# A gated feed-forward stage run in passes of 768 tokens, with fewer weights narrowed in the expert stage before it

## The chip, the cores and the metric

One core of one Trainium2 chip runs the whole program. The metric is the device time of one execution in microseconds; a profiled execution also has a span, the stretch from the first to the last recorded instruction.

## The reference

Three layers follow each other on 2304 tokens of 512 numbers (4 sequences of 576 tokens, 8 heads of 64):

```python
# 1: attention with exponential features (d_feat = 128)
proj = einsum('bhsd,df->bhsf', x, w_phi); proj -= max(abs(proj))
phi = concatenate([exp(proj), exp(-proj)])
num = einsum('bhsf,bhfd->bhsd', phi(q), einsum('bhsf,bhsd->bhfd', phi(k), v))
x = num / (einsum('bhsf,bhf->bhs', phi(q), phi(k).sum(2)) + 1e-6)
# 2: one of 8 experts per token (w1: 512 x 1024, w2: 1024 x 512)
logits = x @ w_gate + modality_bias[modality_id]; e = argmax(logits)
x = gate[e] * (maximum(x @ w1[e], 0) @ w2[e])
# 3: gated stage (w_a, w_b: 512 x 1536, w_out: 1536 x 512)
out = ((x @ w_a) * (x @ w_b)) @ w_out
```

Inputs of attention and of the experts are fp32. The weights of the gated stage come as float64 and are brought to fp32 on the chip, which the kernel calls narrowing.

## The kernel before

**Precision.** Every large product is made of three matmuls in the fp32r format. An operand is split into a rounded part (`...h`, a copy on ScalarE) and a rest (`...l`, a subtraction on VectorE or GpSimd). `mm3` (L51) then adds high by high, high by rest and rest by high: lines L52, L53 and L54 of the profile.

**Attention** (class `Attn`) works in 8 units and writes its result to a DRAM buffer `xs`. While it runs, `Route` sorts the tokens of the first half by expert. Its last matmuls are `nmp` (L236).

**The expert stage** (class `Moe`) works on 4 tiles, two for each half of the tokens. A tile is 608 gathered tokens with the same expert. It has 8 steps (`NJ`), each with 1/8 of the expert's weights and 48 matmuls of 304 columns: steps 0 to 3 make the hidden layer (`l1`, result `hp`, split into `hh` and `hl`, L588 and L589), steps 4 to 7 the second layer (`l2`, result `yp`, copied into `y`, L601). In each step:

- `loadw` (L540) brings raw weights `s` by SP's queue, three buffers (`p_st`); three loads are asked for at the start, and each split asks for the load three steps on.
- `splitw` (L545) makes `wh` on ScalarE (L550) and `wl` (L551) on VectorE in steps 0 to 3, on GpSimd in steps 4 to 7. It is emitted two steps before the weights are used.
- `gather` (L554) fetches 128 tokens by an indirect DMA that GpSimd issues (L559) into one of three buffers (`p_xg`); five make a tile. `transp` (L562) turns them on TensorE (`mxt`, L571) and splits them into `mxh` (ScalarE, L574) and `mxl` (VectorE, L575). The next tile's transposes lie in steps 4 to 7, so the first tile is the only one whose gathers and transposes stand ahead of all expert matmuls.
- `side` holds extra work by step: routing the second half (steps 0 to 6), `close_work` (step 7, gives scratch memory to the narrowing), and from step 8 on `conv(f)` (L901) for ten of the twelve groups (`NPRE = 10`) of gated-stage weights. A group is three pieces of 128x512. `narrow` (L676) takes seven VectorE operations for a piece (L681 to L690) on one pair of scratch tiles, `cvt` and `cvs`; the result `cvo` is stored to the DRAM buffer `wsc`. Groups 0 and 1 are also split here for the first two steps of the next stage. `conv` has a low priority (`LOWP`).

**Between the stages** stands `tc.If(nts[2] > NTMIN)` (L911), for inputs that need more than two tiles in a half. Here it isn't taken, but every engine branches there.

**The gated stage** (class `Moe2`) goes over 6 blocks of 384 tokens and, for each, over 12 groups of weights `f`: 72 steps of 33 matmuls. In a step `ab` (L745) makes two products `abp` (24 matmuls of 384 columns), then `ga` (ScalarE), `gg` (VectorE, L761), `gh` (ScalarE, L762) and `gl` (VectorE, L763); `outp` (L766) of the step before adds to three accumulators `op` (9 matmuls of 512 columns), kept over the 12 groups. `split` (L722) splits the weights of every step anew, 210 pieces in all: `fh` on ScalarE (L728), `fl` (L729) on VectorE for two pieces and on GpSimd for the third. The results `abp` have two buffers each in PSUM (`ps_l2`), the accumulators take three banks. `block` (L733) splits a block of `y` into `yh` and `yl` in the middle of the block before; the first one is split at the head of this stage, behind the If. The two groups that were not narrowed before are narrowed in the first block, and the others are read back from `wsc`. `finish` (L784) scales the result and writes it out by indirect DMA.

**What sets the order.** Code is emitted in the order of these loops; the Tile framework's scheduler then orders each engine's instructions by dependencies and priorities (`LOWP` and `LOWP2` lower the priority of narrowing) and decides on the semaphores. SP's queue carries loads and stores, GpSimd's queue the gathers and the output.

Of the kernel before, what the change touches and what calls it, by code (L numbers as in the profile page):

```python
# [37 lines left out]
NPRE = 10  # L38
CVK = 3
# [478 lines left out]
class Moe:  # L518
    NJ = 8

    def __init__(self, nc, tc, ctx, cst, xs, wm, y, ps_l, ps_t):
# [81 lines left out]
    def run(self, tiles, side={}):  # L603
# [12 lines left out]
        def split(k):  # L616
            if k < NT * NJ:
                self.splitw(get(k // NJ), k % NJ)
                load(k + 3)

        for j in range(3):
            self.gather(get(0), j)
        for k in range(3):
            load(k)
        split(0)
        for j in range(NSUB):
            self.transp(Ts[0], j)
            if j + 3 < NSUB:
                self.gather(Ts[0], j + 3)
        split(1)  # L630
        order = {4: (0,), 5: (1, 2), 6: (3,), 7: (4,)}
        for k in range(NT * NJ):
# [5 lines left out]
            if n + 1 < NT:  # L638
                if j == 2:
                    for i in range(3):  # L640
                        self.gather(get(n + 1), i)
                for i in order.get(j, ()):
                    self.transp(Ts[n + 1], i)
                    if i + 3 < NSUB:
                        self.gather(Ts[n + 1], i + 3)
# [7 lines left out]
class Moe2:  # L653
    NF = FF2 // P

    def __init__(self, nc, tc, w, wsc, y, routes, out, p_w, f64):
        self.nc, self.tc, self.w, self.y, self.routes, self.out = nc, tc, w, y, routes, out
        self.wsc = wsc
        self.p_w, self.f64 = p_w, f64
# [3 lines left out]
    def pools(self, ctx, ps_a, ps_l):  # L663
        tc = self.tc
        pool = lambda n, b: ctx.enter_context(tc.tile_pool(name=n, bufs=b, side="right", reuse_waits="tile"))
        self.p_y = pool("f_y", 6)
# [25 lines left out]
    def early(self, f, pool):  # L692
        nc = self.nc
        tiles = []
        for i in range(3):
            dst = pool.tile([P, 512], F32, tag=f"o{i}", name="cvo")
# [5 lines left out]
            tiles.append(dst)  # L702
        return tiles
# [18 lines left out]
    def split(self, srcs):  # L722
        nc = self.nc
        out = []
        for i, src in enumerate(srcs):
            hi = self.p_w.tile([P, 512], F32R, tag=f"h{i}", name=f"fh{i}")
            lo = self.p_w.tile([P, 512], F32R, tag=f"l{i}", name=f"fl{i}")
            nc.scalar.copy(hi, src)  # L728
            (nc.vector if i < 2 else nc.gpsimd).tensor_sub(lo, src, f32(hi))  # L729
            out.append((hi, lo))  # L730
        return out

    def block(self, bp, blk, n):  # L733
        nc = self.nc
        src = self.y[bp][:, :, blk * n:blk * n + n]
        res = []
        for c in range(4):
            yh = self.p_y.tile([P, n], F32R, tag="h", name="yh")
            yl = self.p_y.tile([P, n], F32R, tag="l", name="yl")
            nc.scalar.copy(yh, src[:, c, :])  # L740
            nc.vector.tensor_sub(yl, src[:, c, :], f32(yh))
            res.append((yh, yl))
# [31 lines left out]
    def run(self, ws, side):  # L774
        nc = self.nc
        n = 384
        blocks = [(bp, b) for bp in range(2) for b in range(HALF // n)]
        y = self.block(*blocks[0], n)
        seq = [(i, f) for i in range(len(blocks)) for f in range(self.NF)]
        prev = None  # L780
        ys = {0: y}
        accs = {}

        def finish(i):  # L784
            bp, b = blocks[i]
# [16 lines left out]
        def second(k):  # L802
            i, f = seq[k]
            if f == 0:
                accs[i] = [self.ps_a.tile([P, 512], F32, tag=f"a{m}", name=f"op{m}") for m in range(n // P)]
            self.outp(gs.pop(k), ws.pop(k), accs[i], f)
# [3 lines left out]
        gs = {}  # L810
        for k, (i, f) in enumerate(seq):
# [25 lines left out]
def trn_kernel(ctx, tc, qk, v, w_phi, mod_id, w_gate, bias, wm, wf, out):  # L837
# [35 lines left out]
    with ExitStack() as mctx:  # L873
# [3 lines left out]
        p_w = ctx.enter_context(tc.tile_pool(name="f_w", bufs=2, **tl))  # L877
        y = [ypool.tile([P, 4, YC], F32, name=f"y{i}") for i in range(2)]
# [107 lines left out]
```

## Time and profile before

| what | value |
|---|---|
| median of 3 runs | 940.4 us (938.87, 940.4 and 945.45) |
| the profiled execution | 943.89 us, its span 942.1 us |
| matmuls, and other instructions | 5861 on TensorE, 15371 in all |
| attention | 0 to about 232 us |
| expert stage, first to last matmul | 240.90 to 471.28 us |
| gated stage, first to last matmul | 477.74 to 934.23 us |

The profile gives for each engine the time in which it was busy, and for TensorE the clock that was granted, as a share of full speed (1.00 is 2.4 GHz, 0.50 is 1.2 GHz; a value between is a mean over a stretch). A busy share tells which engine could be the bound. Which wait costs time is read from the waits and the timeline of a stretch: in brackets stands how long the engine was idle before an instruction and which engine, operand and line ended it. PE is TensorE's matmuls, DVE is VectorE, ACT is ScalarE, POOL is GpSimd; a `q` behind a name is that engine's sequencer.

### The profile page before, as it was taken

Reading aid. Unit: us, or ns where it says so; the run is one execution under the profiler, and the core shown is the slowest. Engines: PE = TensorE matmul, PEld = TensorE weight load, DVE = VectorE, ACT = ScalarE, POOL = GpSimd, SP = SyncE. Lnnn points to the kernel's source line nnn. Section 1 sums busy time; section 2 is a strip of 40 time slices with the busy share of each in tenths; the row PEclk is TensorE's granted clock in tenths of the full one; section 3 lists DMA queues with packets and bytes.
Section 4 is the critical chain, followed back from the end, with each engine's and each line's share of the span. In section 5 each row is a group of like instructions: output and inputs, shape, how many; then the busy total and the mean of one; then the engine's idle time right before and its main releaser. Section 6 shows DMA issues by size and latency. Waiting matters only on the chain. (4 is left out here: it accounts for less than half of the span.)

```text
span 942.1 us, 15371 instructions
## 1 busy us (share of the span) xinstructions
PE 907.3 (96%) x5861; PEld 864.1 (92%) x5861; DVE 622.9 (66%) x1212; ACT 436.2 (46%) x800; POOL 257.3 (27%) x235
## 2 busy tenths in 40 slices
PE   7999999899999989899979999999999999999996
PEld 5899998899999989899979999999999999999996
DVE  7978899979657999999958753353344335334431
ACT  5676765656334433233134454454444445445442
POOL 5444332302241331302103232213213223223122
PEclk7999998799999999899989999999999999999999
DMA  7232330023336566675475000000000000000000
GB/s 249 98 104 79 102 104 13 28 80 106 123 109 205 178 224 204 213 223 180 146 264 198 23 23 12 1 1 34 0 1 35 1 1 34 1 1 34 1 1 34
DMA packets 36291, 81.68 MB, mean 87 GB/s; under 512 B 4688, under 2 KB 14368, under 8 KB 36208
## 3 DMA queue, kind: packets, MB, share of 16 engines
q1 hardware_dynamic: 33168, 70.85, 23.2%
q0 software_dynamic: 3040, 9.75, 3.1%
q8 instruction: 48, 0.79, 0.3%
q14 instruction: 35, 0.29, 0.1%
HBM read 63.29 MB, written 17.30 MB: 86 GB/s over the span
## 5 line engine op out<-in xcount | busy, mean ns | idle before, releaser
L728 ACT CAST fh<-wr 128x512 fp32r<-128x512 f32 x210 | 130.3, 621 | 221.2 <-PE abp L53 147.1
L729 DVE TENSOR_TENSOR fl<-wr,fh 128x512 fp32r<-128x512 f32 x140 | 100.0, 715 | 184.3 <-ACT fh L728 176.2
L52 PE MATMUL abp<-yh,fh 128*128 128x384 f32 x576 | 194.4, 340 | 6.2 <-ACT yh L740 6.2
L53 PE MATMUL abp<-yl,fh 128*128 128x384 f32 x576 | 195.2, 339 | 0.0
L54 PE MATMUL abp<-yh,fl 128*128 128x384 f32 x576 | 194.6, 338 | 0.0
L729 POOL TENSOR_TENSOR fl<-wr,fh 128x512 fp32r<-128x512 f32 x70 | 93.3, 1333 | 340.0 <-ACT fh L728 300.8
L52 PEld LDWEIGHTS abp<-yh,fh 128*128 128x128 f32 x576 | 108.8, 189 | 9.4 <-ACT yh L740 6.4
L53 PEld LDWEIGHTS abp<-yl,fh 128*128 128x128 f32 x576 | 108.6, 189 | 3.0
L54 PEld LDWEIGHTS abp<-yh,fl 128*128 128x128 f32 x576 | 108.6, 188 | 0.0
L52 PE MATMUL op<-fh,gh 128*128 128x512 f32 x216 | 85.5, 396 | 0.0
L53 PE MATMUL op<-fl,gh 128*128 128x512 f32 x216 | 85.1, 394 | 0.0
L54 PE MATMUL op<-fh,gl 128*128 128x512 f32 x216 | 84.5, 394 | 0.0
L53 PE MATMUL yp<-hl,wh 128*128 128x304 f32 x256 | 79.1, 309 | 3.5 <-DVE hl L589 3.5
L52 PE MATMUL yp<-hh,wh 128*128 128x304 f32 x256 | 78.9, 308 | 0.0
L54 PE MATMUL yp<-hh,wl 128*128 128x304 f32 x256 | 78.4, 306 | 0.0
L761 DVE TENSOR_TENSOR gg<-abp,ga 128x384 f32<-128x384 f32 x72 | 40.1, 556 | 57.9 <-PE abp L54 57.5
L53 PE MATMUL hp<-mxl,wh 128*128 128x304 f32 x256 | 77.4, 302 | 0.0
L52 PE MATMUL hp<-mxh,wh 128*128 128x304 f32 x256 | 77.2, 303 | 0.0
L54 PE MATMUL hp<-mxh,wl 128*128 128x304 f32 x256 | 76.8, 300 | 0.0
L236 PE MATMUL nmp<-kx,qts 128*128 128x73 f32 (+1 forms) x640 | 73.4, 271 | 1.9 <-DVE grest L478 1.8
L236 PEld LDWEIGHTS nmp<-kx,qts 128*128 128x128 f32 (+1 forms) x640 | 69.8, 187 | 4.2 <-issue 3.2
L551 POOL TENSOR_TENSOR wl<-s,wh 128x1024 fp32r<-128x1024 f32 x16 | 41.5, 2595 | 110.4 <-ACT wh L550 97.6
(191 smaller groups left out, 1930.6 us busy)
## 6 DMA issues: line engine op xcount, KB each, us to landing
raw<-in_moe_w SPq DMA_DIRECT2D x36, 512.0 KB, 4.6
s<-in_moe_w SPq DMA_DIRECT2D x32, 512.0 KB, 4.2
wsc<-cvo SPq DMA_DIRECT2D x30, 256.0 KB, 4.6
wr<-wsc SPq DMA_DIRECT2D x30, 256.0 KB, 5.4
v<-in_v SPq DMA_DIRECT2D x8, 640.0 KB, 5.3
qk<-in_qk SPq DMA_DIRECT2D x7, 640.0 KB, 5.0
qk<-in_qk SPq DMA_DIRECT2D x8, 512.0 KB, 6.0
xs<-x SPq DMA_DIRECT2D x16, 256.0 KB, 2.5
```

Of the source, the lines that this page charges most:

```text
L52: nc.tensor.matmul(out, lh, rh, start=start, stop=False)
L53: nc.tensor.matmul(out, lh, rl, start=False, stop=False)
L54: nc.tensor.matmul(out, ll, rh, start=False, stop=stop)
L236: nc.tensor.matmul(ps[pp, o, :], qt[:, c, a, pp], st["kx", b][:, 2 * h + c, :], start=c == 0, stop=c == 1)
L551: (nc.gpsimd if j >= 4 else nc.vector).tensor_sub(lo, src, f32(hi))
L728: nc.scalar.copy(hi, src)
L729: (nc.vector if i < 2 else nc.gpsimd).tensor_sub(lo, src, f32(hi))
L761: nc.vector.tensor_mul(g, pss[1][:, :n], a)
```

## The change

- **Gated stage in passes.** A pass takes two blocks, 768 tokens. The loops run over pass, group and the block within the pass, so weights are split once for a pass and used for two steps: 108 pieces in place of 210. The steps stay 72 of 33 matmuls.
- **PSUM.** Two blocks need six banks of accumulators; `abp` is left with one buffer each (`ps_l2`, 2 to 1).
- **Rests on VectorE.** `wl` of steps 4 to 7 and the third `fl` of each step go from GpSimd to VectorE.
- **Narrowing.** Six groups, not ten, are narrowed in the expert stage; the other six (18 pieces) follow in the first pass, one piece after each step or nearly so. The scratch there has one buffer, not two. `cvo` has two buffers for all pieces, and the pieces of groups 0 and 1 are split as soon as each is made.
- **Buffers.** The raw expert weights (`p_st`) and the gathers (`p_xg`) have two buffers each in place of three; loads and gathers are asked for two ahead. The next tile's transposes 0 and 1 lie in step 4, 2 in step 5.
- **The first block of y** is split ahead of the If, into a pool of 8 buffers that is made early; inside the If, behind the extra tiles, it is split again. The other blocks are split at the first step that needs them or, at a pass's end, ahead of it.

```diff
-NPRE = 10
-CVK = 3
+NPRE = 6
...
-        self.p_st = pool("m_st", 3, **r)
+        self.p_st = pool("m_st", 2, **r)
-        self.p_xg = pool("m_xg", 3, **r)
+        self.p_xg = pool("m_xg", 2, **r)
...
-        (nc.gpsimd if j >= 4 else nc.vector).tensor_sub(lo, src, f32(hi))
+        nc.vector.tensor_sub(lo, src, f32(hi))
...
-                load(k + 3)
+                load(k + 2)
-        for j in range(3):
+        for j in range(2):
             self.gather(get(0), j)
-        for k in range(3):
+        for k in range(2):
             load(k)
         split(0)
         for j in range(NSUB):
             self.transp(Ts[0], j)
-            if j + 3 < NSUB:
-                self.gather(Ts[0], j + 3)
+            if j + 2 < NSUB:
+                self.gather(Ts[0], j + 2)
         split(1)
-        order = {4: (0,), 5: (1, 2), 6: (3,), 7: (4,)}
+        order = {3: (), 4: (0, 1), 5: (2,), 6: (3,), 7: (4,)}
...
-            (nc.vector if i < 2 else nc.gpsimd).tensor_sub(lo, src, f32(hi))
+        nc.vector.tensor_sub(lo, src, f32(hi))
...
-        seq = [(i, f) for i in range(len(blocks)) for f in range(self.NF)]
+        seq = [(p, f, i) for p in range(0, nb, 2) for f in range(self.NF) for i in (p, p + 1)]
...
-        for k, (i, f) in enumerate(seq):
+        for k, (p, f, i) in enumerate(seq):
             with self.tc.high_priority(offset=-LOWP2):
                 for st in side.get(k, ()):
                     st()
-            if k + 1 < len(seq) and k + 1 not in ws:
-                ws[k + 1] = self.split(self.res[seq[k + 1][1]])
-            if f == 6 and i + 1 < len(blocks):
-                ys[i + 1] = self.block(*blocks[i + 1], n)
-            gs[k] = self.ab(ys[i], ws[k])
+            if i == p + 1 and k + 1 < len(seq):
+                nxt = seq[k + 1][:2]
+                if nxt not in ws:
+                    ws[nxt] = [self.split(j, src) for j, src in enumerate(self.res[nxt[1]])]
+                if nxt[0] != p:
+                    ys[p + 2] = self.block(p + 2)
+            if i not in ys:
+                ys[i] = self.block(i)
+            gs[k] = self.ab(ys[i], ws[p, f])
...
         mo.run(tiles, side)
+        ys = {0: m2.block(0)}
         with tc.If(nts[2] > NTMIN):
             for rt, nt in zip(routes, nts):
                 extra(tc, mo, rt, nt)
+            m2.block(0, ys[0])
         rctx.close()
-    cv.append(ctx.enter_context(tc.tile_pool(name="cv2", bufs=2, **tl)))
+    cv.append(ctx.enter_context(tc.tile_pool(name="cv2", bufs=1, **tl)))
...
-    for f in range(2, NPRE):
-        side.setdefault(max(f - 4, 0), []).extend(late[f])
-    for f in range(2):
-        side.setdefault(8, []).extend(late[f])
-    for j, st in enumerate(late[f] for f in range(NPRE, Moe2.NF)):
-        side.setdefault((j * CVK) // 2 + 1, []).extend(st)
+    for f in range(NPRE):
+        side.setdefault(2 * f - 4 if f > 1 else 16, []).extend(late[f])
+    for f in range(NPRE, Moe2.NF):
+        n = len(late[f])
+        for i, st in enumerate(late[f]):
+            side.setdefault(1 + 3 * (f - NPRE) + 3 * i // n, []).append(st)
...
-    ps_l = ctx.enter_context(tc.tile_pool(name="ps_l2", bufs=2, space=PSUM, **tl))
+    ps_l = ctx.enter_context(tc.tile_pool(name="ps_l2", bufs=1, space=PSUM, **tl))
```

The line numbers of the changed kernel are 1 lower from L52 to the expert stage's end and a few lower behind it (L571 becomes L570, L729 becomes L725, L761 becomes L756).

Three places show what the scheduler makes of it. The first is TensorE's row where attention ends and the expert stage begins: `nmp` are attention's last matmuls, `mxt` the transposes of the gathered tokens (4 per gather), `hp` the first expert matmul. Before:

```order
L236 MATMUL nmp<-kx,qts 128x73 x5
L571 MATMUL mxt<-ident,xg 128x128 x8
L236 MATMUL nmp<-kx,qts 128x73 x8
L571 MATMUL mxt<-ident,xg 128x128 x4
L236 MATMUL nmp<-kx,qts 128x73 x8
L236 MATMUL nmp<-kx,qts 64x73 x8
L571 MATMUL mxt<-ident,xg 128x128 x4
L571 MATMUL mxt<-ident,xg 128x96 x4
L52 MATMUL hp<-mxh,wh 128x304
```

And the same place now:

```order
L235 MATMUL nmp<-kx,qts 128x73 x5
L570 MATMUL mxt<-ident,xg 128x128 x8
L235 MATMUL nmp<-kx,qts 128x73 x16
L570 MATMUL mxt<-ident,xg 128x128 x8
L235 MATMUL nmp<-kx,qts 64x73 x8
L570 MATMUL mxt<-ident,xg 128x96 x4
L51 MATMUL hp<-mxh,wh 128x304
```

The third and the fourth gather are turned behind 16 more matmuls of attention, where it was 8 and 24, and 8 matmuls of attention stand between the fourth and the last, which may only be fetched when the third has been turned.

The second is GpSimd's row through the first half of the expert stage, with its gathers (`xg`) and the rests `wl`. Before:

```order
L559 DMA xg<-xs_63,idx_2902 128x512 x4
L559 DMA xg<-xs_63,idx_2902 96x512
L559 DMA xg<-xs_63,idx_2902 128x512 x3
L551 TENSOR_TENSOR wl<-s,wh 128x1024 x2
L559 DMA xg<-xs_63,idx_2902 128x512
L551 TENSOR_TENSOR wl<-s,wh 128x1024
L559 DMA xg<-xs_63,idx_2902 96x512
L551 TENSOR_TENSOR wl<-s,wh 128x1024
```

Now nothing stands between the gathers of the four tiles:

```order
L558 DMA xg<-xs_63,idx_2898 128x512 x4
L558 DMA xg<-xs_63,idx_2898 96x512
L558 DMA xg<-xs_63,idx_2898 128x512 x4
L558 DMA xg<-xs_63,idx_2898 96x512
L558 DMA xg<-xs_64,idx_3928 128x512 x4
L558 DMA xg<-xs_64,idx_3928 96x512
```

GpSimd does no arithmetic here any more; what it did stands in VectorE's row.

The third is VectorE's row over one step in the gated stage's narrowing, from one product `gg` to the next; `wr` is a narrowed piece, `fl` a rest of weights, `cvs` and `cvt` the scratch. Before:

```order
L761 TENSOR_TENSOR gg<-abp,ga 128x384
L690 TENSOR_TENSOR wr_2_14776<-cvt,cvs 128x512
L729 TENSOR_TENSOR fl_15218<-wr_1_14766,fh_15217 128x512
L687 TENSOR_SCALAR cvs<-cvt 128x512
L763 TENSOR_TENSOR gl<-gg,gh 128x384
L681 TENSOR_SCALAR cvs<-raw 128x512
L688 SCALAR_TENSOR_TENSOR cvs<-raw,cvs 128x512
L682 TENSOR_SCALAR cvs<-cvs 128x512
L690 TENSOR_TENSOR wr_0_14777<-cvt,cvs 128x512
L729 TENSOR_TENSOR fl_15285<-wr_0_14768,fh_15284 128x512
L683 TENSOR_SCALAR cvt<-cvs 128x512
L761 TENSOR_TENSOR gg<-abp,ga 128x384
```

Now:

```order
L756 TENSOR_TENSOR gg<-abp,ga 128x384
L684 SCALAR_TENSOR_TENSOR cvt<-raw,cvt 128x512
L758 TENSOR_TENSOR gl<-gg,gh 128x384
L686 TENSOR_SCALAR cvs<-cvt 128x512
L687 SCALAR_TENSOR_TENSOR cvs<-raw,cvs 128x512
L725 TENSOR_TENSOR fl_14849<-wr_2_14619,fh_14848 128x512
L689 TENSOR_TENSOR wr_0_14632<-cvt,cvs 128x512
L680 TENSOR_SCALAR cvs<-raw 128x512
L725 TENSOR_TENSOR fl_14964<-wr_0_14620,fh_14963 128x512
L681 TENSOR_SCALAR cvs<-cvs 128x512
L682 TENSOR_SCALAR cvt<-cvs 128x512
L756 TENSOR_TENSOR gg<-abp,ga 128x384
```

The mixture of narrowing, rests and `gg` is much the same; but it lasts for 18 narrowings where there were 6, and the operations of two pieces no longer alternate.

## Rows read from the trace of the kernel before

**Rows 1.** The page's first part: busy us, share of the span, instructions.

```profile
PE 907.3 (96%) x5861; PEld 864.1 (92%) x5861; DVE 622.9 (66%) x1212; ACT 436.2 (46%) x800; POOL 257.3 (27%) x235
```

**Rows 2.** Stretches: us, then PE, PEld, DVE, ACT, POOL busy (x), PEclk, DMA, GB/s.

```profile
332.00:344.00 12.00, 9.98 (x72) 9.55 (x72) 11.60 (x17) 5.12 (x9) 6.56 (x5) 1.00 0.69 224
...
380.00:392.00 12.00, 8.86 (x58) 8.61 (x57) 11.76 (x21) 3.04 (x6) 3.50 (x3) 0.88 0.53 171
392.00:404.00 12.00, 12.00 (x78) 12.00 (x77) 11.59 (x18) 2.77 (x6) 3.31 (x2) 0.83 0.64 209
...
476.00:488.00 12.00, 10.26 (x49) 10.27 (x50) 5.16 (x10) 5.25 (x12) 0.00 (x0) 0.78 0.79 276
...
554.00:630.00 76.00, 76.00 (x399) 71.10 (x398) 31.95 (x53) 35.73 (x67) 18.81 (x16) 1.00 0.03 11
```

**Rows 3.** Waits of TensorE, 188 to 500 us: us in total, times, longest.

```profile
PE yp L53 <- DVE hl L589: 3.5, 2, 3.1
...
PE mxt L571 <- DVE mxl L575: 2.0, 1, 2.0
```

**Rows 4.** Timeline, 384 to 390 us: start, us, engine line operation [idle before].

```profile
384.70 3.29 DVE L685 SCALAR_TENSOR_TENSOR cvt<-raw,cvt 128x512 int32<-128x512 int32 x1
...
385.06 2.38 POOL L551 TENSOR_TENSOR wl<-s,wh 128x1024 fp32r<-128x1024 f32 x1
...
387.92 0.46 DVE L589 SCALAR_TENSOR_TENSOR hl<-hp,hh 128x304 fp32r<-128x304 f32 x1
...
389.88 0.62 PE L53 MATMUL yp<-hl,wh 128*128 128x304 f32 x1 [3.14 <-DVE hl L589]
```

**Rows 5.** Timeline, VectorE from 456 to 461 us: the last operations of two narrowings.

```profile
456.50 0.69 DVE L690 TENSOR_TENSOR cvo<-cvt,cvs 128x512 f32<-128x512 f32 x1
...
460.52 0.69 DVE L690 TENSOR_TENSOR cvo<-cvt,cvs 128x512 f32<-128x512 f32 x1
```

**Rows 6.** Groups by line and form: count, busy us, mean ns, idle before.

```profile
L729 DVE TENSOR_TENSOR fl<-wr,fh 128x512 fp32r<-128x512 f32 x140 | 100.0, 715 | 184.3 <-ACT fh L728 176.2 <-DMA wr<-wsc 5.1 <-PE abp L54 3.0
...
L551 POOL TENSOR_TENSOR wl<-s,wh 128x1024 fp32r<-128x1024 f32 x16 | 41.5, 2595 | 110.4 <-ACT wh L550 97.6 <-DVE tv L407 12.8
...
L763 DVE TENSOR_TENSOR gl<-gg,gh 128x384 fp32r<-128x384 f32 x72 | 41.2, 572 | 1.2 <-ACT gh L762 1.2
...
L761 DVE TENSOR_TENSOR gg<-abp,ga 128x384 f32<-128x384 f32 x72 | 40.1, 556 | 57.9 <-PE abp L54 57.5 <-issue 0.2
...
L551 DVE TENSOR_TENSOR wl<-s,wh 128x1024 fp32r<-128x1024 f32 x16 | 19.4, 1220 | 2.3 <-ACT wh L550 2.3
```

**Rows 7.** Timeline, 231 to 243 us: TensorE and GpSimd where the experts begin.

```profile
232.35 1.04 PE L571 MATMUL mxt<-ident,xg 128*128 128x128 f32 x8
...
233.23 0.94 POOL L559 DMA_INDIRECT xg<-xs,idx  x1 [4.74 <-PE mxt L571]
...
239.80 1.32 PE L571 MATMUL mxt<-ident,xg 128*128 128x128 f32 x8 [1.42 <-DMA xg<-xs,idx]
...
240.90 0.39 PE L52 MATMUL hp<-mxh,wh 128*128 128x304 f32 x1
```

**Rows 8.** All 20 gathers into the tile xg, from issue to landing.

```profile
DMA to landing us min/median/max: 3.1/4.7/8.1
```

**Rows 9.** Timeline, 463.5 to 490 us: TensorE and ScalarE between the stages.

```profile
471.28 0.30 PE L54 MATMUL yp<-hh,wl 128*128 128x304 f32 x1
...
477.17 2.58 ACT L740 CAST yh<-y 128x384 fp32r<-128x384 f32 x6 [5.08 <-DVEq L911]
...
477.74 1.65 PE L52 MATMUL abp<-yh,fh 128*128 128x384 f32 x4 [6.15 <-ACT yh L740]
```

**Rows 10.** Line 911, the If: engine, count, ns min/median/max, first and last start.

```profile
L911 ACTq EVENT_SEMAPHORE  x2: 17/17/17, 475.5 to 475.5; - x2
...
L911 ACTq COMPARE_BRANCH  x1: 50/50/50, 472.7 to 472.7; - x1
...
L911 DVEq EVENT_SEMAPHORE  x1: 21/21/21, 477.0 to 477.0; - x1
```

More of the change, by code (lines that the diff above doesn't have):

```diff
@@ L639, in run @@
                 if j == 2:
-                    for i in range(3):
+                    for i in range(2):
                         self.gather(get(n + 1), i)
@@ L643, in run @@
                     self.transp(Ts[n + 1], i)
-                    if i + 3 < NSUB:
-                        self.gather(Ts[n + 1], i + 3)
+                    if i + 2 < NSUB:
+                        self.gather(Ts[n + 1], i + 2)
             if j < 4:
@@ L690, in narrow, with early @@
         nc.vector.tensor_add(dst, t.bitcast(F32), s.bitcast(F32))
-    def early(self, f, pool):
+    def early(self, f, pool, parts):
         nc = self.nc
-        tiles = []
         for i in range(3):
-            dst = pool.tile([P, 512], F32, tag=f"o{i}", name="cvo")
+            dst = pool.tile([P, 512], F32, tag="o", name="cvo", bufs=2)
             if self.f64:
@@ L701, in early @@
             nc.sync.dma_start(out=self.wsc[f][:, 512 * i:512 * i + 512], in_=dst)
-            tiles.append(dst)
-        return tiles
+            if parts is not None:
+                parts.append(self.split(i, dst))
     def late_steps(self, f, pool, wres):
@@ L720, in late_steps, with split, block @@
         return steps
-    def split(self, srcs):
+    def split(self, i, src):
         nc = self.nc
[L724 to L728, printed above, removed]
-            (nc.vector if i < 2 else nc.gpsimd).tensor_sub(lo, src, f32(hi))
[L730 to L734, printed above, removed]
+        hi = self.p_w.tile([P, 512], F32R, tag=f"h{i}", name=f"fh{i}")
+        lo = self.p_w.tile([P, 512], F32R, tag=f"l{i}", name=f"fl{i}")
+        nc.scalar.copy(hi, src)
+        nc.vector.tensor_sub(lo, src, f32(hi))
+        return hi, lo
+    def block(self, i, res=None):
+        nc, n = self.nc, self.N
+        bp, blk = divmod(i, HALF // n)
         src = self.y[bp][:, :, blk * n:blk * n + n]
[L736 to L739, printed above, removed]
+        if res is None:
+            res = [[self.p_y.tile([P, n], F32R, tag=t, name=nm) for t, nm in (("h", "yh"), ("l", "yl"))]
+                   for c in range(4)]
+        for c, (yh, yl) in enumerate(res):
             nc.scalar.copy(yh, src[:, c, :])
             nc.vector.tensor_sub(yl, src[:, c, :], f32(yh))
-            res.append((yh, yl))
         return res
@@ L772, in outp, with run @@
             mm3(nc, acc[m], gh[:, ms], gl[:, ms], wh, wl, f == 0, f == self.NF - 1)
[L774 to L778, printed above, removed]
-        seq = [(i, f) for i in range(len(blocks)) for f in range(self.NF)]
-        prev = None
-        ys = {0: y}
-        accs = {}
+    def run(self, ws, ys, side):
+        nc, n = self.nc, self.N
+        nb = NTOK // n
+        seq = [(p, f, i) for p in range(0, nb, 2) for f in range(self.NF) for i in (p, p + 1)]
+        accs, gs = {}, {}
         def finish(i):
-            bp, b = blocks[i]
+            bp, b = divmod(i, HALF // n)
             for m, acc in enumerate(accs.pop(i)):
@@ L802, in second @@
         def second(k):
-            i, f = seq[k]
+            p, f, i = seq[k]
             if f == 0:
-                accs[i] = [self.ps_a.tile([P, 512], F32, tag=f"a{m}", name=f"op{m}") for m in range(n // P)]
-            self.outp(gs.pop(k), ws.pop(k), accs[i], f)
+                accs[i] = [self.ps_a.tile([P, 512], F32, tag=f"a{i - p}{m}", name=f"op{m}") for m in range(n // P)]
+            self.outp(gs.pop(k), ws[p, f], accs[i], f)
             if f == self.NF - 1:
                 finish(i)
-        gs = {}
-        for k, (i, f) in enumerate(seq):
+        for k, (p, f, i) in enumerate(seq):
             with self.tc.high_priority(offset=-LOWP2):
@@ L902, in conv @@
             with tc.high_priority(offset=-LOWP):
-                done = m2.early(f, cv[0])
                 if f < 2:
-                    ws[f] = m2.split(done)
+                    ws[0, f] = []
+                m2.early(f, cv[0], ws.get((0, f)))
         K0 = 8
```

13 lines of the change are left out of this document (7 added, 6 removed).

## The prediction

> **What bounds the kernel now.** I read the busy shares first, then the busy times in stretches, then what TensorE waited for, and then the timeline around each of those waits. The reader is to see that TensorE is busy for 907.3 of 942.1 us [rows 1]: whatever the change does to the other engines counts only where TensorE stops, or where its clock is halved.
>
> The stretches [rows 2] show where that is. In the gated stage (554 to 630 us) TensorE is busy for 76.00 of 76.00 us at full clock. The 399 matmuls of that stretch are 12.1 steps of 33, so a step takes 6.29 us. VectorE, ScalarE and GpSimd have room there, and no wait of TensorE is on record. In the expert stage VectorE is the engine without room: 11.76 of 12 us from 380 on, and 11.60 of 12 from 332 on, and there TensorE loses time. The waits give the sums: 3.5 us for the rest `hl` of the expert's hidden layer, 2.0 us for the rest `mxl` of the gathered tokens, both made on VectorE [rows 3]. The timeline of the longest of them shows the cause [rows 4]: GpSimd begins a `wl` rest at 385.06 and runs 2.38 us; the VectorE operation that began just before it lasts 3.29 us, where the other two-input operations of the narrowing take 0.69 [rows 5]; TensorE starts again only at 389.88, after 3.14 us of idling. Then the clock: the mean grant of 0.88 and 0.83 in the stretches from 380 to 404 [rows 2] is 2.9 + 4.1 = 7.0 us at the lower level (1.2 GHz), of which about 6.3 us (389.9 to some 396.2) is work at half speed, worth about 3.2 us. After the idle stretch of 2.0 us (the stretch 332 to 344 has it) the grant is 1.00. So the expert stage loses 3.5 + 2.0 + 3.2 = 8.7 us behind VectorE.
>
> The last loss is between the stages [rows 9]: the last expert matmul starts at 471.28, the first gated one at 477.74, after 6.15 us, and it waits for `yh`. ScalarE makes `yh` only when VectorE has reported past the If: 477.0. ScalarE itself branched at 472.7 and reported at 475.5 [rows 10]. In the stretch 476 to 488 the grant is 0.78, so 5.3 us at 1.2 GHz, to about 481.3: 3.6 us of work at half speed.
>
> **The change part by part.**
>
> Narrowing six groups in the expert stage, not ten, takes 12 of 30 narrowings off VectorE there. One takes 4.02 us from its last operation to that of the next [rows 5]: 48 us. The 16 `wl` rests that come over from GpSimd cost 16 x 1.22 = 19.5 us [rows 6]. Net 29 us less in a stage of 230 (from 240.90 [rows 7] to 471.28 [rows 9]), and the holds by GpSimd go with its 16 rests (2.6 us each): VectorE falls from full to well under. So I let the 8.7 us go, and give 1.0 us back for waits that stay: in the first four steps of a tile VectorE still has a rest of weights, four `hl` and three quarters of a narrowing per step. Ends: all 8.7 gained, or half. Term: -7.7.
>
> Two gather buffers, not three, cost at the one place where TensorE has nothing else: the first tile. The order shows it: before, four matmul groups of transposes can run as soon as two late gathers land; now the last of five gathers is issued only when the third transpose has read its buffer. In the trace the gather of 233.23 is read at 239.80, TensorE waiting the last 1.42 us, and the experts begin at 240.90 [rows 7]. Three loads of weights were on the DMA engines at once then, now two, so I put the third transpose at about 237.5, its end at 238, and the last gather at 238 plus the median landing of 4.7 us [rows 8]: 242.7, the experts at 243.1, 2.2 us late. With the shortest landing of 3.1 it is 0.6 late, with the longest of 8.1, 5.6. TensorE idles some 2.8 us meanwhile (a rest of attention fills 1 us). Idling 2.0 us left the clock up and 3.14 us took it down [rows 2 to 4]; 2.8 is nearer to the second, so I add the 3.2 us that this cost there. Term: +5.4, ends +0.6 and +8.8. In the later tiles a step (230 us over 32, 7.2 us) covers the median landing, and only the longest would show.
>
> The Trainium skill (DMA: Bandwidth & Descriptors, section on the anatomy of one DMA on the GpSimd path) fits such a transfer as 2.0 us plus its bytes over 436 GB/s; for 256 KB that is an estimate of 2.6 us. By it the experts would begin on time, the clock would stay up, and the term would be about 0; the shortest landing of the trace, 3.1, lies above it and the median far above, so the rows are used.
>
> Two staging buffers of expert weights, not three: a load now starts two steps ahead of its split, and the split runs two steps ahead of its use. Hidden by two steps of 7.2 us; nothing. The four y splits ahead of the If lie beside expert matmuls on ScalarE and VectorE; nothing.
>
> At the If the first gated matmul no longer waits for a `yh` made behind it, but its counters still include what ScalarE and VectorE report past the branch. VectorE comes early now (its last work is a `wl`), ScalarE cannot: it must copy the last expert result. So TensorE starts at about 475.6 in place of 477.74. That stretch is at 1.2 GHz on the trace, so 2.1 us earlier is worth 1.1. Ends: 0, or 2.5 if the clock comes back as much earlier. Term: -1.1.
>
> The Trainium skill (Advanced Engine Details and Errata, section Control Flow Timing) gives a compare-and-branch some 108 ns. By it TensorE would go on at about 472.3 with its clock up, and the term would be near -7; here ScalarE's branch to its next report is 2.8 us [rows 10], and the row is used.
>
> In the gated stage the matmuls are the same: 72 steps of 33. Splitting weights once per pass halves the splits (210 casts to 108), on engines that hold nobody there: nothing. What it adds is load on VectorE while the other 18 narrowings run, about 17 steps. Per step: 18/17 x 4.02 = 4.26 for narrowing, gg and gl 0.556 + 0.572, 1.5 weight rests x 0.715 = 1.07 [rows 5, 6], together 6.46 against 6.29 us of TensorE. VectorE falls behind by 17 x 0.17 = 2.9 us. Each step's product `gg` now has one accumulator where it had two: it must be read before the second half of the next step's first layer starts, 21 of 33 matmuls or two thirds of a step later (by columns), 4.2 us. 2.9 is under that: nothing. Ends: -0 and, if the narrowing and its one pair of scratch tiles run at 7.0 us a step, the price of the third rival. The y splits at the two pass borders have a full step each.
>
> **The sum.** -7.7 + 5.4 - 1.1 = -3.4 us. The profiled execution took 943.89 us, span 942.1 and 1.8 around it: 940.5 by this sum. The median of the runs shown is 940.4, 3.5 below the profiled one, so I forecast 937 us.
>
> **The rivals.**
>
> First, a cheap start: the last gather lands in 3.1 to 3.5 us, TensorE idles under 2 us and keeps its clock, and the expert stage gives all 8.7. Then 0.6 - 8.7 - 1.1 to 2.5 = -9 to -11: 930 us. For it speaks that the competing loads are fewer; against it the median of 4.7 over 20 gathers. The page's 2.6 us belongs here.
>
> Second, the stalls stay: `hl` and `mxl` come late for queueing behind narrowings that a scheduler places, not for GpSimd. Then only half the 8.7 returns, the start costs 5.4 to 8.8, and the clock falls again: about +2 to +4, 943 us. Against it: each long VectorE operation of these rows lies over a GpSimd rest.
>
> Third, slower: VectorE becomes the bound of the first pass. Place: steps 1 to 17 of the gated stage. Each narrowing there works on one pair of scratch tiles, so each of its operations waits for the last, and each must wait for raw weights in two buffers. At 7.0 us a step the lag is 17 x 0.7 = 12 us, less the 4.2 that one accumulator allows: 8 us of stalls, and one or two falls of the clock at 3.2: 11 to 14 us, 948 to 951. It decides from 6.54 us a step on (6.29 + 4.2/17). Against it: the sum of 6.46 already takes every operation at its full length.
>
> Fourth, that the change does nothing for the expert stage because something else had been waited for: the waits name no other engine, so I give it nothing of its own.
>
> **How the numbers follow.** The forecast (933 to 941 us) has 0.55, the cheap start 0.18, the stalls that stay 0.15, VectorE as the bound 0.12. A measurement of this kernel tells about 1%, 9.4 us, from no change: faster by that means under 931.0, which most of the cheap start reaches, 0.14; slower means over 949.8, part of the third rival and what I have not thought of, 0.10; the rest, 0.76, is within. The range goes from 928 to 947: it holds all of the forecast and the stalls, most of the cheap start, and leaves out the worse half of the third.
>
> **What would show it.** Right: no GpSimd arithmetic after attention; VectorE under 10.5 of 12 us between 300 and 460; no TensorE wait over 1 us for `hl` or `mxl` after the first tile; before the first expert matmul a TensorE wait of 2 to 4 us for the gather and a grant of 0.5 for some us; the first gated matmul some 4 us after the last expert one; full clock and 6.3 us a step from there. Wrong: waits of TensorE for `gg` or `fl` in the first 17 gated steps; or a gap at the If as long as before.

## The result, and the profile after

The changed kernel takes 931.25 us (median of 4 runs, 929.87 to 933.54) against 941.49 us of the kernel before on the same chip: a ratio of 0.989, 95% interval 0.9847 to 0.9934. That is 10.2 us less. The forecast was 937, its range 928 to 947.

The page's first part, busy time and share by engine, shows what moved (to be read beside [rows 1]):

```profile
PE 895.7 (96%) x5861; PEld 855.4 (92%) x5861; DVE 580.3 (63%) x1192; ACT 375.2 (40%) x692; POOL 120.5 (13%) x147
```

GpSimd's work fell by half, VectorE's by 43 us, although VectorE took over GpSimd's rests. The number of matmuls is the same and TensorE still fills 96%.

The stretches of the changed kernel that answer to [rows 2] (the same columns):

```profile
332.00:344.00 12.00, 12.00 (x89) 12.00 (x89) 11.18 (x21) 4.06 (x8) 0.96 (x1) 1.00 0.80 234
...
380.00:392.00 12.00, 12.00 (x90) 12.00 (x89) 10.71 (x20) 3.09 (x6) 1.95 (x3) 1.00 0.85 268
392.00:404.00 12.00, 12.00 (x91) 12.00 (x90) 10.75 (x19) 4.30 (x8) 0.00 (x0) 1.00 0.68 193
...
464.00:476.00 12.00, 11.92 (x53) 11.72 (x54) 8.56 (x19) 4.64 (x10) 0.00 (x0) 0.78 0.89 307
```

TensorE is now full at full clock through the expert stage; only the first stretch of the gated stage still has a clock below 1.00. The waits of TensorE from 188 to 500 us, which answer to [rows 3], hold nothing of the expert stage any more:

```profile
PE abp L51 <- ACTq L907: 3.7, 1, 3.7
PE mxt L570 <- DMA xg<-xs,idx: 2.7, 2, 2.2
PE mxt L570 <- DVE rec L245: 1.1, 1, 1.1
PE kvp L52 <- DVE kl L167: 0.3, 1, 0.3
```

To see where the time went, the span is cut at the starts of five matmuls that the timeline gives: the last `kvp` of attention (some `nmp` follow it, to 238.4 us in the kernel before), the first `hp`, the last `yp`, the first `abp`, and the last `op`. All runs of this study, in us (the last column is the ratio to the kernel before, with its interval):

| kernel | last kvp at | kvp to hp | hp to yp | yp to abp | abp to last op | to the end | ratio |
|---|---|---|---|---|---|---|---|
| before | 225.7 | 15.2 | 230.4 | 6.5 | 456.5 | 7.8 | |
| changed | 221.5 | 17.4 | 221.2 | 4.0 | 454.3 | 10.0 | 0.989 (0.9847, 0.9934) |
| e1 no If | 225.9 | 17.3 | 222.4 | 0.1 | 451.9 | 10.0 | 0.9848 (0.9823, 0.9873) |
| e2 y late | 224.4 | 17.6 | 223.2 | 4.6 | 457.8 | 10.0 | 0.9958 (0.994, 0.9977) |
| e3 one PSUM buffer | 225.5 | 14.1 | 230.0 | 5.8 | 458.2 | 7.8 | 0.9996 (0.9974, 1.0019) |
| e4 tail | 225.1 | 17.4 | 222.1 | 4.2 | 453.5 | 7.9 | 0.9883 (0.9857, 0.9909) |
| e5 wl on GpSimd | 219.7 | 18.1 | 224.7 | 4.0 | 453.6 | 10.0 | 0.9953 (0.9939, 0.9967) |
| e6 ten groups | 224.9 | 17.6 | 224.1 | 4.0 | 453.3 | 10.0 | 0.9925 (0.9897, 0.9953) |
| e7 before, six | 224.7 | 15.1 | 230.0 | 5.0 | 471.3 | 7.8 | 1.0127 (1.0099, 1.0155) |
| e8 before, wl on VectorE | 222.6 | 15.2 | 221.3 | 4.8 | 456.8 | 8.1 | 0.9879 (0.9855, 0.9902) |
| e9 three edits | 225.1 | 21.3 | 222.3 | 4.0 | 453.6 | 8.3 | 0.9932 (0.9906, 0.9958) |
| e10 two gathers | 225.8 | 15.4 | 232.4 | 6.1 | 457.2 | 7.8 | 1.0019 (0.9999, 1.0038) |
| e11 two loads | 220.3 | 14.5 | 229.1 | 7.1 | 457.1 | 7.8 | 0.9992 (0.997, 1.0014) |
| e12 two edits | 223.7 | 14.4 | 221.3 | 4.8 | 454.7 | 8.2 | 0.9878 (0.9855, 0.99) |

The changed kernel's span is 13.7 us shorter: -4.2 in attention, +2.2 at the experts' start, -9.2 in the expert stage, -2.5 at the If, -2.2 in the gated stage, +2.2 at the end. The part in attention is not the change's: the order of TensorE's instructions there is the same in both up to the gathers' transposes, and the other kernels reach the last `kvp` anywhere from 219.7 to 225.9. Without it 9.5 us are left, near the 10.2 of the medians.

### The profile page after: what moved, and what is told of

Same layout as the page of the kernel before. It is cut to its first block, busy times and chain, and to the rows that moved or that the text cites. A ratio compares the mean times of both kernels' runs of the same rounds, so it can differ in the third digit from the quotient of the medians.

```text
span 928.4 us, 14869 instructions
## 1 busy us (share of the span) xinstructions
PE 895.7 (96%) x5861; PEld 855.4 (92%) x5861; DVE 580.3 (63%) x1192; ACT 375.2 (40%) x692; POOL 120.5 (13%) x147
## 5 line engine op out<-in xcount | busy, mean ns | idle before, releaser
L52 PE MATMUL abp<-yl,fh 128*128 128x384 f32 x576 | 194.0, 337 | 0.0
L756 DVE TENSOR_TENSOR gg<-abp,ga 128x384 f32<-128x384 f32 x72 | 40.1, 557 | 151.4 <-PE abp L53 151.2
L52 PEld LDWEIGHTS abp<-yl,fh 128*128 128x128 f32 x576 | 109.0, 189 | 3.1
L725 DVE TENSOR_TENSOR fl<-wr,fh 128x512 fp32r<-128x512 f32 x102 | 70.2, 688 | 58.5 <-ACT fh L724 56.0
L724 ACT CAST fh<-wr 128x512 fp32r<-128x512 f32 x102 | 63.3, 621 | 106.9 <-PE abp L52 76.9
L785 POOL DMA_INDIRECT out<-o,perm x18 | 18.7, 1039 | 518.0 <-ACT o L784 287.0
L52 PE MATMUL op<-fl,gh 128*128 128x512 f32 x216 | 85.0, 394 | 0.0
L755 ACT COPY ga<-abp 128x384 f32<-128x384 f32 x72 | 34.3, 476 | 111.2 <-PE abp L53 108.7
L52 PE MATMUL yp<-hl,wh 128*128 128x304 f32 x256 | 77.6, 303 | 0.0
L52 PE MATMUL hp<-mxl,wh 128*128 128x304 f32 x256 | 77.3, 303 | 0.0
L757 ACT CAST gh<-gg 128x384 fp32r<-128x384 f32 x72 | 37.0, 514 | 87.6 <-DVE gg L756 87.3
```

The source lines that it names most:

```text
L52: nc.tensor.matmul(out, lh, rl, start=False, stop=False)
L725: nc.vector.tensor_sub(lo, src, f32(hi))
L755: nc.scalar.copy(a, pss[0][:, :n])
L756: nc.vector.tensor_mul(g, pss[1][:, :n], a)
L757: nc.scalar.copy(gh, g)
L785: st = nc.gpsimd.indirect_dma_start(out=self.out[:, :], out_offset=bass.IndirectOffsetOnAxis(ap=self.routes[bp].perm[:, c:c + 1], axis=0), ...
```

## The experiments

**Who held VectorE in the expert stage?** The theory: GpSimd's rests `wl` stretch VectorE's operations beside them. The rival: there was too much narrowing. Four runs take the two edits apart, in the changed kernel (e5, e6) and in the one before (e7, e8).

```diff
 # e5 (changed kernel) and, the other way round, e8 (kernel before)
-        nc.vector.tensor_sub(lo, src, f32(hi))
+        (nc.gpsimd if j >= 4 else nc.vector).tensor_sub(lo, src, f32(hi))
 # e6 (changed kernel) and, the other way round, e7 (kernel before)
-NPRE = 6
+NPRE = 10
```

e5, expected: 

> The changed kernel with the rests wl of steps 4 to 7 on GpSimd again, nothing else. The expert stage, first to last matmul, is 230.4 us before and 221.2 us after. If GpSimd's rests holding VectorE's operations made the stalls, waits of TensorE for hl or mxl of 1 us or more come back and the stage takes 224 to 229 us. If the amount of narrowing made them, six groups leave VectorE free enough: no such wait, 221 to 223 us, and the time stays within 1 us of the changed kernel.

e6, expected: 

> The changed kernel with ten groups narrowed in the expert stage, nothing else; the rests stay on VectorE. If the amount of narrowing made the stalls: VectorE is full (it gets 48 us of work back in a stage of 221), waits for hl or mxl return, 226 to 231 us for the expert stage. If GpSimd's rests made them: 221 to 223 us, VectorE full but nobody waiting more than 0.5 us.

e7, expected: 

> The kernel before with six groups narrowed in the expert stage, not ten, nothing else. If the amount of narrowing made the stalls: 221 to 223 us for the expert stage in place of 230.4, no wait for hl or mxl over 0.5 us, and VectorE early at the If, so a gap between the stages of 4.6 us in place of 6.5; the time falls by 8 to 11 us. If GpSimd's rests made them: 225 to 229 us with waits of 1 us or more left, the gap still 4.6.

e8, expected: 

> The kernel before with the rests wl of steps 4 to 7 on VectorE, nothing else. If GpSimd's rests made the stalls: 221 to 224 us for the expert stage, VectorE full without TensorE waiting. If the amount of work on VectorE made them, 20 us more of it (16 of 1.22 us) make them worse: 231 to 245 us, and the gap at the If 6 us or more.

The waits of TensorE for the expert stage's tiles, first in e5, then in e7 (its gated stage too):

```profile
PE yp L52 <- DVE hl L588: 0.9, 1, 0.9
```

```profile
PE op L52 <- ACT gh L762: 5.4, 2, 4.0
PE abp L52 <- DVE wr L690: 4.7, 1, 4.7
PE abp L52 <- ACT fh L728: 4.3, 3, 1.9
PE yp L53 <- DVE hl L589: 3.5, 3, 1.6
PE mxt L571 <- DVE mxl L575: 2.3, 2, 2.0
```

In e8 no wait for `hl` or `mxl` is on record, with ten groups and 19.5 us more arithmetic on VectorE: 221.3 us, what the whole change has. e7 has six groups, and its expert stage has the waits and the length of the kernel before. So the rests on GpSimd made the stalls, and the amount of narrowing did not. e5 agrees only weakly: its expert stage is 3.5 us longer than the changed kernel's, but 1.7 of that is a fall of the clock at its start (the rows stand under "Start" below), and the one wait is 0.9 us, just under the 1 us expected. The rests do hold VectorE there as in e7: in both, eight operations of narrowing last 2.3 to 3.3 us, each over a rest on GpSimd. What TensorE loses by that, 0.9 us of waits in e5 and 5.8 in e7, must hang on what stands behind a held operation; no run separates that. e6 is a miss by its length, 224.1 us where 221 to 223 was expected, but not because of narrowing: no wait over 0.2 us is on record inside its expert stage, and 5.7 us at half clock at its start are worth 2.8.

The groups by form tell it without any wait: mean ns of one is the second number behind the bar. VectorE from 241 to 460 us in the kernel before:

```profile
L685 DVE SCALAR_TENSOR_TENSOR cvt<-raw,cvt 128x512 int32<-128x512 int32 x27 | 29.2, 1080 | 0.6
L688 DVE SCALAR_TENSOR_TENSOR cvs<-raw,cvs 128x512 f32<-128x512 uint32 x27 | 21.2, 785 | 0.7
L690 DVE TENSOR_TENSOR cvo<-cvt,cvs 128x512 f32<-128x512 f32 x26 | 20.2, 779 | 0.6
L687 DVE TENSOR_SCALAR cvs<-cvt 128x512 int32<-128x512 int32 x27 | 20.1, 746 | 0.5
```

and in e8:

```profile
L551 DVE TENSOR_TENSOR wl<-s,wh 128x1024 fp32r<-128x1024 f32 x29 | 35.5, 1224 | 12.7 <-ACT wh L550 12.4 <-DMA wsc<-cvo 0.3
...
L688 DVE SCALAR_TENSOR_TENSOR cvs<-raw,cvs 128x512 f32<-128x512 uint32 x27 | 18.6, 689 | 0.6
L690 DVE TENSOR_TENSOR cvo<-cvt,cvs 128x512 f32<-128x512 f32 x27 | 18.6, 689 | 0.7
L685 DVE SCALAR_TENSOR_TENSOR cvt<-raw,cvt 128x512 int32<-128x512 int32 x27 | 18.6, 688 | 0.5
...
L687 DVE TENSOR_SCALAR cvs<-cvt 128x512 int32<-128x512 int32 x27 | 11.4, 424 | 0.6
```

The three two-input operations take 688 to 689 ns without GpSimd's rests beside them and 779 to 1080 with them: 10.6 + 2.6 + 2.4 = 15.6 us over 27 narrowings. A one-input operation (`L687`) is held as well, 746 against 424 ns, which is 8.7 us more. So moving the rests cost VectorE 19.5 us and gave some 24 back, and what mattered, no single operation is held for 3 us any more. In the expert stage of the kernel before, 12 of 208 operations of narrowing take 2.2 to 3.3 us, and each of them runs beside a rest on GpSimd. `hl` and `mxl`, for which TensorE waits, are not held themselves: the eight that run beside a rest keep their 0.47 and 0.69 us. They come late because they queue behind a held narrowing, as in [rows 4].

e7 is slower by 1.3% for another reason: the late schedule of the kernel before puts the 18 pieces into steps 1, 2, 4, 5, 7 and 8, three at a time, and TensorE waits 5.4 us for `gh` and 4.3 for `fh`, and the clock falls once more (3.4 us at 544.8): 471.3 us for the gated stage. (The wait for `wr` is its gap at the If.)

**What is the gap at the If?**

```diff
 # e1
-        with tc.If(nts[2] > NTMIN):
-            for rt, nt in zip(routes, nts):
-                extra(tc, mo, rt, nt)
-            m2.block(0, ys[0])
 # e2 (and f_y taken at the head of the gated stage)
-        ys = {0: m2.block(0)}
-            m2.block(0, ys[0])
-    m2.run(ws, ys, side)
+    m2.run(ws, {}, side)
```

e1, expected: 

> The changed kernel without the If and its body (the code for inputs with extra tiles is left out; it isn't run for this input). If the branch itself makes the gap between the stages: the gap from the last expert matmul to the first gated one, 3.96 us in the changed kernel, falls under 0.5 us, the clock stays at 2.4 GHz through it (in the changed kernel about 5 us after it are at 1.2 GHz, worth 2.5 us), so some 6 us in all and a time near 925. If the gap waits for the split of y, or for scratch memory that changes hands, it stays over 2 us and the time falls by 2 us at most.

e2, expected: 

> The changed kernel with the first block of y split behind the If, as before, and its eight buffers taken at the head of the gated stage, so at other addresses (near those of the kernel before). Two questions. The gap: if splitting ahead of the If shortened it, it goes back from 3.96 to 6 us or more; if VectorE's early end did (it reaches the If 18 us ahead of ScalarE in the changed kernel), the gap grows only by a cast and a subtraction, to 4.5 to 5 us. The pitch of a gated step, 6.32 us before and 6.28 after: if the addresses of y make the difference, it goes back to 6.32 (3 us over 72 steps); if the PSUM banks or the number of weight splits make it, it stays at 6.28.

In the changed kernel the last copy of the expert stage (`L600`) and line 907, now the If's, show who is last (timeline, then the line's instructions with ns and start):

```profile
460.51 0.41 ACT L600 COPY y<-yp 128x304 f32 x1 [2.98 <-PE yp L53]
...
464.08 0.69 PE L51 MATMUL abp<-yh,fh 128*128 128x384 f32 x1 [3.66 <-ACTq L907]
```

```profile
L907 ACTq EVENT_SEMAPHORE  x2: 17/17/17, 464.0 to 464.1; - x2
...
L907 DVEq EVENT_SEMAPHORE  x1: 21/21/21, 445.7 to 445.7; - x1
```

VectorE passed the If 18 us ahead; ScalarE can branch only behind its last copy and reports 2.5 us after its branch at 461.5. Without the If the gap is 0.1 us and the clock stays up, so the gated stage is 2.4 us shorter: the branch costs 3.8 + 2.4 = 6.2 us in these two traces. The median, 928.46, is 3 us above the 925 expected, within what the intervals of the two ratios allow. With y split behind the If (e2) the gap is 4.6, not 6: of the 2.5 us won there 0.6 belong to the split ahead and 1.9 to VectorE reaching the If before ScalarE. e7 and e8, where it does that too and y is split behind the If, have 5.0 and 4.8 us. The sizes are rough: with the code before it the gap goes from 5.8 to 7.1 us (before, e3, e10, e11).

**Why is every gated step shorter?** A step was forecast unchanged, at 6.29 us; that is a count over a stretch whose ends cut matmuls. The first `abp` of two successive steps, in the kernel before, the changed one and e2:

```profile
704.84 0.34 PE L52 MATMUL abp<-yh,fh 128*128 128x384 f32 x1
...
711.15 0.34 PE L52 MATMUL abp<-yh,fh 128*128 128x384 f32 x1
```

```profile
703.03 0.34 PE L51 MATMUL abp<-yh,fh 128*128 128x384 f32 x1
...
709.31 0.34 PE L51 MATMUL abp<-yh,fh 128*128 128x384 f32 x1
```

```profile
704.60 0.34 PE L51 MATMUL abp<-yh,fh 128*128 128x384 f32 x1
...
710.91 0.34 PE L51 MATMUL abp<-yh,fh 128*128 128x384 f32 x1
```

6.31, 6.28 and 6.31 us; over 37 steps it is 6.320, 6.280 and 6.320. TensorE waits for nothing there; it is 0.040 x 72 = 2.9 us. e2 has the passes and one split per pass, but y lies at byte addresses 131040 to 155616 of a partition, much as in the kernel before (137184 to 155616); in the changed kernel it is at 92000 to 116576. In the built programs `gh` and `gl` move with it: they begin at 131040 before, at 124896 in e2 and at 149472 in the changed kernel. e3 tests another candidate.

```diff
-    ps_l = ctx.enter_context(tc.tile_pool(name="ps_l2", bufs=2, space=PSUM, **tl))
+    ps_l = ctx.enter_context(tc.tile_pool(name="ps_l2", bufs=1, space=PSUM, **tl))
```

e3, expected: 

> The kernel before with one PSUM buffer each for the two products of a gated step, not two, nothing else. If the number of banks that the products go round sets the pitch of a step, it falls from 6.32 to 6.28 us and the time by 3 us; if y's addresses or the weight splits set it, the pitch stays at 6.32 us. If one buffer is late for TensorE, waits of the products for VectorE appear and the pitch grows.

It stays at 6.320: not the banks.

**The end.**

```diff
 # e4
+        t = len(seq) - 3
+        seq[t], seq[t + 1] = seq[t + 1], seq[t]
-            if i == p + 1 and k + 1 < len(seq):
+            if k + 1 < len(seq):
```

e4, expected: 

> The changed kernel with two steps of the last pass exchanged: the first block's twelfth group before the second block's eleventh, so that the first block is finished one step (6.3 us) earlier. If the six stores that GpSimd issues one after the other (1.28 us each) make the end of the changed kernel, 10.0 us from the last matmul to the end of the span, longer than that of the kernel before, 7.9 us, the end is 7.9 us again and the time 2.1 us less. If the end waits for the landing of the last store alone, it stays at 10.0 us.

GpSimd's stores, the first and the last of six, in the changed kernel and in e4 (start, us):

```profile
916.70 0.97 POOL L785 DMA_INDIRECT out<-o,perm  x1 [140.26 <-ACT o L784]
...
923.12 0.97 POOL L785 DMA_INDIRECT out<-o,perm  x1 [0.30 <-ACT o L784]
```

```profile
914.31 0.97 POOL L787 DMA_INDIRECT out<-o,perm  x1 [133.98 <-ACT o L786]
...
924.90 0.97 POOL L787 DMA_INDIRECT out<-o,perm  x1 [0.30 <-issue]
```

In the changed kernel two blocks end together: the first of six stores starts 1.7 us before the last matmul (918.40), the last one 4.7 us behind it. In e4 three are gone before the last matmul, at 922.3, and the end is 7.9 us. The profile shows the 2.1 us; the median, 931.94, doesn't (929 was expected), since such a difference is under its interval (0.5%).

**The start of the experts.**

```diff
 # e10: gathers two ahead (with the loops over 2, as in the change)
-        self.p_xg = pool("m_xg", 3, **r)
+        self.p_xg = pool("m_xg", 2, **r)
 # e11: loads two ahead (in the loop at the start too)
-        self.p_st = pool("m_st", 3, **r)
+        self.p_st = pool("m_st", 2, **r)
```

e10, expected: 

> The kernel before with two gather buffers, not three, nothing else. From the last kvp matmul of attention to the first expert matmul it is 15.2 us before (14.1 to 15.2 over four runs of kernels that share this code) and 17.4 after (17.3 to 18.1 over six). If the gather buffers make the difference: 17 us or more, with a wait of TensorE for the last gather of 2 us. If the two weight loads do: 14 to 15.5 us.

e11, expected: 

> The kernel before with two buffers for the raw expert weights, not three, nothing else. If the gather buffers make the late start, from the last kvp matmul to the first expert matmul it stays at 14 to 15.2 us, or gets shorter, as one load less is under way beside the gathers. If the loads do: 17 us or more. The expert stage stays at 230 us if a load two steps ahead is early enough; waits for wh or wl show if it isn't.

By the cut at the first `hp` e10 is a miss, 15.4 us; but there the last transposes stand behind the first expert matmuls, and to the last `yp` it takes 15.4 + 232.4 = 247.8 us where the kernel before takes 245.6. So two gather buffers cost some 2 us, and two load buffers nothing (14.5 + 229.1 = 243.6). This is one trace of each: the four kernels with three gather buffers and GpSimd's rests (before, e3, e7, e11) take 243.6 to 245.6.

**A kernel that keeps the gains alone.**

```diff
 # e9 and e12: wl on VectorE as in e8, f_y no longer taken with the gated stage's pools; then e9
 # (left out: cvo with two buffers, the pieces of groups 0 and 1 split one by one, the split inside the If):
+        m2.p_y = ctx.enter_context(tc.tile_pool(name="f_y", bufs=6, **tl))
+        y0 = m2.block(0, 0, 384)
         with tc.If(nts[2] > NTMIN):
 # e12: the pool of y behind the late scratch
+    ctx.enter_context(tc.tile_pool(name="pad", bufs=1, **tl)).tile([P, 512], F32, name="pad")
+    m2.p_y = ctx.enter_context(tc.tile_pool(name="f_y", bufs=6, **tl))
```

e9, expected: 

> The kernel before with three things: the rests wl of steps 4 to 7 on VectorE; y's six split buffers taken early, so at the lower addresses that they have in the changed kernel (room for them comes from cvo with two buffers, each piece of groups 0 and 1 split as soon as it is made); and the first block of y split ahead of the If. Blocks of 384 tokens, ten groups in the expert stage and three gather buffers stay. If the runs so far are read rightly: 221 to 222 us for the expert stage, a gated step of 6.28 us in place of 6.32 (3 us), an end of 7.9 us, and 0.6 us less between the stages, so 3.5 us under the kernel with wl on VectorE alone (928.9): 925.4, and 5 to 6 under the changed kernel. If the pitch comes from the passes and not from the addresses: 6.32 us and 928.

e12, expected: 

> The kernel before with two things: the rests wl of steps 4 to 7 on VectorE, and y's six split buffers on the other side of the memory, behind the late scratch, at byte addresses 110432 to 128864 of a partition in place of 137184 to 155616 (a pad of 2 KB keeps them off memory that the narrowing's stores still read). Attention's end and its gathers are as in the kernel before. If y's addresses set the pitch: 6.28 us a gated step in place of 6.32, so 3 us under the kernel with wl on VectorE alone (928.9), 926, and 5 under the changed kernel. If the pitch comes from something else that changed with y's place in the two kernels with 6.28: 6.32 us and 928 to 929.

e9 takes 936.51 us where 925.4 was expected. It has what was expected of each stage, or within 1 us of it, but for the start, 21.3 us, and the clock behind it. GpSimd's row there:

```profile
225.52 0.25 POOL L319 IOTA i<- 128x128 f32 x1 [38.89 <-PE kvp L54]
...
227.72 1.06 POOL L559 DMA_INDIRECT xg<-xs,idx  x1 [0.84 <-DVE tokp L345]
```

In e8 the first gather starts at 212.65. The memory taken early for y pushed the routing's tables onto tiles that attention still used (in the built program from 92000 to 110432, over attention's `v` and `vl`); GpSimd waited for those with the tables' constants, and the gathers stand behind them in its queue. TensorE then waited 2.8 us, and the clock was at 0.50 from 236 to 248 us. The changed kernel takes y early as well, and its first gather starts late too, 1.6 us before the last `kvp` in place of 10.0; but the two first gathers still land before their transposes begin, and e2, with y late, starts its experts no sooner (17.6 us).

In e12, where y takes its place late, the start is 14.4 us and the step 6.280. Its median, 928.86, is that of e8 to the digit where 926 was expected: the 2.9 us of the pitch are less than the two intervals can tell. In the profiles its gated stage is 2.1 us shorter than e8's, with 1.4 us more at half clock behind the If. Both are level with the changed kernel or a little under it; a clear win over it was not shown.

## Why the prediction was right, and where its terms were off

The direction and the range held; the likeliest case did not. The number that came is that of the first rival, the cheap start at 930, but by its whole 8.7 us and its clock, not by its reason: the last gather landed in 3.6 us, not 3.1 to 3.5, and TensorE idled 2.7 us for gathers, not under 2. Term by term, from the table:

- **Expert stage, -7.7.** Measured -9.2: all 8.7 us of stalls and clock went, and nothing had to be kept back. Of the two reasons given, GpSimd's holds are what e7 and e8 show; the 48 us of narrowing that the change takes off were no part of it. One sign failed: VectorE was to be under 10.5 of 12 us, and from 332 to 404 us it is still at 10.7 to 11.2, with nobody waiting. The Trainium skill (SBUF — State Buffer, section Who interferes with whom) says that a VectorE instruction with two inputs in this memory contends with a GpSimd instruction that reads it. The 1080 against 688 ns agree.
- **Start, +5.4.** This is the term that was off most, in one of its two parts. That the experts begin 2.2 us late was right: 17.4 us after the last `kvp` in place of 15.2. The fall of the clock, 3.2 us, did not come in the traced execution. The transposes of the changed kernel and what TensorE waited for there:

```profile
229.09 3.69 PE L235 MATMUL nmp<-kx,qts 128*128 128x73 f32 x32
233.93 0.63 PE L570 MATMUL mxt<-ident,xg 128*128 128x128 f32 x4 [1.15 <-DVE rec L245]
235.09 0.63 PE L570 MATMUL mxt<-ident,xg 128*128 128x128 f32 x4 [0.54 <-DMA xg<-xs,idx]
235.65 0.79 PE L235 MATMUL nmp<-kx,qts 128*64 128x73 f32 x16
238.60 0.53 PE L570 MATMUL mxt<-ident,xg 96*128 96x96 f32 x4 [2.17 <-DMA xg<-xs,idx]
```

The 2.8 us of idling that were forecast came in two pieces, 0.54 and 2.17, with attention's last matmuls between them, and the clock stayed up. That was in part luck. Five other runs share this start, and in four of them the clock fell. The stretch around the first `hp` in the changed kernel, e1, e2, e4, e5 and e6 (columns of [rows 2]; the clock is the third figure from the end):

```profile
236.00:248.00 12.00, 9.83 (x82) 9.71 (x78) 7.69 (x26) 4.04 (x9) 1.91 (x2) 1.00 0.28 84
```

```profile
238.00:250.00 12.00, 10.24 (x68) 9.51 (x69) 7.60 (x28) 2.65 (x6) 2.84 (x3) 0.72 0.45 133
```

```profile
238.00:250.00 12.00, 10.25 (x67) 9.93 (x68) 7.01 (x25) 2.57 (x7) 2.76 (x3) 0.72 0.35 104
```

```profile
238.00:250.00 12.00, 9.21 (x78) 8.95 (x79) 7.71 (x28) 3.42 (x8) 2.83 (x3) 1.00 0.39 122
```

```profile
238.00:250.00 12.00, 12.00 (x78) 12.00 (x76) 6.64 (x23) 4.07 (x9) 0.95 (x1) 0.86 0.11 29
```

```profile
238.00:250.00 12.00, 9.44 (x59) 9.18 (x60) 6.70 (x23) 2.31 (x6) 2.73 (x3) 0.72 0.37 114
```

Behind the first `hp` that is 2.7 us at half clock in e1, 4.6 in e2, 3.4 in e5 and 5.7 in e6, worth 1.3 to 2.8 us. By about that the expert stages of e1, e2 and e6 are longer than 221.2 us; in e5 it is half of it. So the term took as certain what comes in four of six traces, and its 3.2 us are above every price seen in the stage. How long TensorE idles does not settle it: e1 idled 0.8, 0.9 and 0.8 us and its clock fell, e4 idled 0.9, 0.5 and 2.4 us and kept it. Two errors within the 2.2 us cancelled: counted from the last `kvp`, the last gather was issued 1.0 us later than put, mostly because the third transpose ended 0.7 us late, and it landed in 3.6 us, not in the median of 4.7.

- **If, -1.1.** Measured -2.5 in the gap, but 5.1 us at half clock behind it where it was 3.6, which takes 0.8 back: -1.7. e4, e5, e6 and e9, with the same gap or nearly, have 2.8 to 3.4 us there. ScalarE was last, as forecast.
- **Gated stage, nothing.** VectorE did keep up: no wait of TensorE behind the first gated matmul, so the third rival fell; e7 shows what it looks like when it comes, 14.8 us, near the 11 to 14 worked out for it. What was not seen was the pitch, -2.9, and the six stores at the end, +2.2; the two nearly cancel, which is luck as well.

The sum from the terms is -9.2 + 2.2 - 1.7 - 2.9 + 2.2 = -9.4, against -3.4 forecast. Half of the difference is the clock at the start, in the traced execution. The second rival, that the stalls stay, fell: no wait for `hl` or `mxl` is left in the changed kernel, nor in e8.

## What to carry to other kernels

Look at the mean time of one operation by form before blaming an engine's load: a VectorE operation whose mean lies well above its shortest may be held by a neighbour, and moving the neighbour's work onto the same engine can be the cure. One edit of this change, a single line, is worth as much as all of it. Where a change frees or takes buffers, ask which queue waits for that memory and what stands behind it.

## What was not expected

- The pitch of the same matmuls goes with where tiles lie: 6.320 us a step in the seven kernels with y from 131040 up, 6.280 in the seven with y below 128864. e8 and e12, one of each, have the same order of TensorE's instructions. That y's address is the cause is not shown, since `gh` and `gl` move with it. Some three quarters of the 0.040 us lie in the 24 `abp` (176.1 to 174.7 ns from one to the next); the rest lies in the `op` (233.2 to 232.2), which don't read y. Why is open.
- The same wait can cost the clock or not. TensorE's wait for `mxl` near 340 us is 2.0 to 2.1 us long in the kernel before, e3, e7, e10 and e11; the clock fell behind it for 3.4 us in e3, e7 and e10 and stayed up in the other two. So the forecast's reading, that 2.0 us leave it up, rested on one trace.
- Attention, with the same order of TensorE's instructions, ended up to 6 us apart. The stretch 120 to 160 us in the kernel before and in the changed one (columns of [rows 2]):

```profile
120.00:160.00 40.00, 38.19 (x327) 37.22 (x328) 37.48 (x86) 26.01 (x47) 11.70 (x10) 0.91 0.20 65
```

```profile
120.00:160.00 40.00, 37.85 (x351) 36.81 (x350) 38.79 (x95) 26.33 (x48) 13.73 (x9) 1.00 0.19 61
```

An idle stretch of 1.81 us for the same tile (`grest`) cost the clock in the one and not in the other: 6.8 us at half clock, worth 3.4 us.
